# Softplus in one activation, exponentials in groups, and a new order for an attention and MLP kernel

## The chip, the cores and the metric

The kernel runs on one core of a Trainium2 chip. The metric is the device time of one execution in microseconds (us). Below, PE is TensorE, DVE VectorE, ACT ScalarE, POOL GpSimd and SP SyncE, which here only issues DMAs.

## The reference

Eight batches of eight heads: tokens `x` (512 x 64 a head) and a state (32 x 64 a head) read each other by softmax attention. The 544 rows of each batch go through a two-layer MLP whose activation is softplus.

```python
scores = scale * np.matmul(x, state.transpose(0, 1, 3, 2))       # x reads the state
a = np.exp(scores - scores.max(-1, keepdims=True)); a /= a.sum(-1, keepdims=True) + 1e-09
xread = np.matmul(a, state)
scores2 = scale * np.matmul(state, x.transpose(0, 1, 3, 2))      # the state reads x
a2 = np.exp(scores2 - scores2.max(-1, keepdims=True)); a2 /= a2.sum(-1, keepdims=True) + 1e-09
sread = np.matmul(a2, x)
rows = np.concatenate([xread, sread], axis=2)                    # -> (4608, 512)
h = rows @ w_in                                                  # 512 x 2048
g = np.maximum(h, 0.0) + np.log1p(np.exp(-np.abs(h)))            # softplus
out = g @ w_out                                                  # 2048 x 512
```

The weights come as 64-bit floats, and the kernel turns them into 32-bit ones on the chip.

## The kernel before, in words

Most products are made exact enough by splitting each fp32 operand into a high part (a cast to fp32r) and a low part (the rest) and adding three products, `PASSES` (line 27): high by high, high by low, low by high. `split` (line 86) does this: the cast on ACT or POOL, the subtraction on DVE or POOL; the table `MOVED` (line 40) says which. The early score products, the products with the weights and the transposes run in plain fp32.

The attention of the tokens is folded into the weights: V = state x w_in (per batch and head) is made first, so that GEMM 1 multiplies the transposed attention weights `aT` by V (`gemm1`, line 471: six products of 512 columns into one of two PSUM banks `h`). `softplus` (line 460) turns the tile into g: Abs, Exp and Ln on ACT, then max(h, 0) + t on DVE, and a split into `ghi` and `glo`, three buffers each. `gemm2` (line 482) adds twelve products into four banks `acc`. One tile of 128 columns of w_in is a slot; there are 16 slots a batch, and `flush` (line 545) runs a slot's GEMM 2 once three slots are pending. The state's rows of all batches go through the same MLP together near the end (`gemm1_read`, line 518), and the last batch closes the run.

`as_f32` (line 104) converts a weight piece: Prelu on ACT makes the high word (line 111), DVE shifts the low word (line 114) and joins the two (line 115). `make_v0` makes the first 512 columns of V for batches 0 to 3 from half-width pieces (lines 158 and 167), `make_vf` the others (lines 200 and 211), and `make_v` those of the later batches. `attention` is a generator of steps named by a letter and a head group 0 or 1: Q scores (line 341), A a transposition, M maximum, subtraction and exponential, N normalisation, D the transposed weights `aT`, E the exponential of the state's scores, G its transposes on PE (line 392), R the reading of x by the state (line 405), X its scaling. Batches 0 and 1 run in plain fp32 (`whole`), the others with split operands.

The order is written out by hand in strings that `run` (line 603) reads: `START` for batches 0 and 1 with all weight preparation, a `BLOCK` for each batch from 2 on, `LAST` for the last. `|` is a slot of GEMM 1, `g` a flush, `a b c` a step of attention of a batch, `v V U` steps of V, `W` a w_out piece, `i o` a load ahead, `p F` a split or a load of V. `LOADS` sets the first loads and `ATT` the order of the steps. A scheduler then places the instructions on each engine's queue; each engine works its queue in order, and all DMAs are issued from SP's queue.

Of the kernel before, what the change touches and what calls it, by code (L numbers as in the profile page):

```python
# [47 lines left out]
def attention_then_softplus_mlp(ctx: ExitStack, tc, xn, xt, zq, zp, stk, w_in, w_out, out):  # L48
# [55 lines left out]
    def as_f32(t, tag="wt"):  # L104
        if t.dtype != I64:
            return t
        v = t.bitcast(I32).rearrange("p (n t) -> p n t", t=2)
# [8 lines left out]
        return r
# [595 lines left out]
```

## Time and profile before

| | us |
|---|---|
| median of 3 runs | 708.37 (706.07 to 711.12) |
| the profiled execution | 708.3, span 706.3 |
| PE, ACT, DVE, POOL busy | 680.7, 501.3, 466.3, 172.8 |
| mean granted clock of PE | 0.995 |

The span runs from the first to the last instruction of the trace. Busy time is the union of an engine's instructions; a matmul's end is modelled. The granted clock is a share of 2.4 GHz, so 0.50 is 1.2 GHz. In an x count a plain fp32 product stands as two records.

### The profile page before, as it was taken

What the parts mean: (1) busy time and instruction counts of PE and PEld (TensorE: products, weight loads), DVE (VectorE), ACT (ScalarE), POOL (GpSimd) and SP (SyncE); (2) the same over time, 40 slices, a digit from 0 to 9 for tenths busy, and PEclk for the clock granted to TensorE, in tenths of its full rate; (3) what the DMA queues carried; (4) which work ended last, traced back from release to release, by engine and by line L of the source; (5) the groups of instructions that cost most, each with busy time, mean ns of one, the idle gap of its engine ahead of it and who ended that gap; (6) DMA issues with size and microseconds to landing.
All of it is one profiled execution on the core that took longest, in us unless ns stands there. A gap on an engine that the chain in (4) does not pass through costs nothing.

```text
span 706.3 us, 9196 instructions
## 1 busy us (share of the span) xinstructions
PE 680.7 (96%) x3012; PEld 536.0 (76%) x3012; DVE 466.3 (66%) x818; ACT 501.3 (71%) x914; POOL 172.8 (24%) x170
## 2 busy tenths in 40 slices
PE   5679999999999999999999999999999999999997
PEld 2455666888877878778777887888788888888876
DVE  4499768936798997796858754875487534544322
ACT  2588988766588778799878856875687556657452
POOL 1221102665233565201201070107010510000220
PEclk9999999999999999999999999999999999999999
DMA  8768896221335456354433311320111013412001
GB/s 267 239 246 287 265 306 199 74 61 48 96 104 164 149 162 204 105 198 153 132 92 108 103 52 38 104 75 14 47 60 59 5 58 104 143 52 60 1 0 59
DMA packets 42063, 82.91 MB, mean 117 GB/s; under 512 B 6176, under 2 KB 13088, under 8 KB 42016
## 3 DMA queue, kind: packets, MB, share of 16 engines
q1 hardware_dynamic: 42016, 82.33, 36.3%
q8 instruction: 23, 0.38, 0.2%
q14 instruction: 24, 0.20, 0.1%
HBM read 56.62 MB, written 25.69 MB: 117 GB/s over the span
## 4 chain that ended last, share of the span: by engine, by line
PE 81%; ACT 9%; DVE 7%; issue 2%; DMA 1%; POOL 0%; SPq 0%; ACTq 0%; DVEq 0%; POOLq 0%
PE acc L485 47%; PE h L478 22%; PE h L525 3%; PE aux L235 2%; PE aux L411 1%; ACT t L463 1%; ACT t L462 1%; ACT t L464 1%; ACT ghi L90 1%; PE aux L341 1%; PE aux L347 1%; DVE k L91 1%; PE aux L392 1%; DMA xT<-in_xt_dram 1%; PE aux L200 1%
## 5 line engine op out<-in xcount | busy, mean ns | idle before, releaser
L485 PE MATMUL acc<-wout,ghi 128*128 128x512 f32 x1088 | 343.1, 394 | 0.9 <-DVE StK L577 0.5
L485 PEld LDWEIGHTS acc<-wout,ghi 128*128 128x128 f32 x1088 | 203.2, 188 | 48.2 <-issue 2.4
L485 PE MATMUL acc<-wout,glo 128*128 128x512 f32 x544 | 214.1, 394 | 0.0
L478 PE MATMUL h<-aT,vhl 128*128 128x512 f32 x768 | 203.7, 402 | 4.3 <-DVE t L465 3.8
L478 PEld LDWEIGHTS h<-aT,vhl 128*128 128x128 f32 x768 | 142.2, 189 | 44.4 <-DVE t L465 9.6
L465 DVE SCALAR_TENSOR_TENSOR t<-h,t 128x512 f32<-128x512 f32 x136 | 93.1, 686 | 97.4 <-ACT t L464 97.1
L462 ACT ACTIVATE t<-h 128x512 f32<-128x512 f32 x136 | 81.4, 598 | 77.4 <-DVE glo L91 37.7
L485 PEld LDWEIGHTS acc<-wout,glo 128*128 128x128 f32 x544 | 102.1, 188 | 22.7 <-issue 0.7
L91 DVE TENSOR_TENSOR glo<-t,ghi 128x512 fp32r<-128x512 f32 x100 | 70.3, 703 | 35.4 <-ACT ghi L90 14.8
L90 ACT CAST ghi<-t 128x512 fp32r<-128x512 f32 x104 | 64.5, 620 | 36.4 <-PE acc L485 23.2
L464 ACT ACTIVATE t<-t 128x512 f32<-128x512 f32 x136 | 86.2, 634 | 2.8
L463 ACT ACTIVATE t<-t 128x512 f32<-128x512 f32 x136 | 86.3, 634 | 2.2
L91 DVE TENSOR_TENSOR vhl<-vf,vhl 128x512 fp32r<-128x512 f32 x62 | 47.1, 760 | 36.0 <-ACT vhl L90 34.0
L83 POOL TENSOR_SCALAR ghi<-t 128x512 fp32r<-128x512 f32 x32 | 21.7, 679 | 180.7 <-PE acc L485 139.8
L91 POOL TENSOR_TENSOR glo<-t,ghi 128x512 fp32r<-128x512 f32 x36 | 48.5, 1351 | 49.6 <-ACT ghi L90 43.1
L90 ACT CAST vhl<-vf 128x512 fp32r<-128x512 f32 x59 | 36.4, 616 | 18.1 <-PE h L525 11.7
L368 POOL TENSOR_TENSOR T<-T,sm 128x512 f32<-128x512 f32 x13 | 15.1, 1160 | 120.7 <-DVE sm L367 92.3
L111 ACT ACTIVATE k<-k 128x512 f32<-128x512 f32 (+1 forms) x32 | 20.2, 645 | 10.3 <-DMA k<-in_w_in_dram 7.7
L525 PEld LDWEIGHTS h<-sreadT,vhl 128*128 128x128 f32 x192 | 23.6, 191 | 2.4 <-DVE t L465 2.2
L525 PE MATMUL h<-sreadT,vhl 128*128 128x256 f32 x192 | 24.9, 286 | 0.1
L352 DVE TENSOR_TENSOR k<-aux,k 64x512 f32<-64x512 f32 x24 | 16.4, 682 | 12.5 <-ACT k L351 12.3
L115 DVE SCALAR_TENSOR_TENSOR wt<-k,wt 128x512 int32<-128x512 int32 (+1 forms) x26 | 20.2, 791 | 2.0 <-ACT k L111 1.7
(161 smaller groups left out, 697.6 us busy)
## 6 DMA issues: line engine op xcount, KB each, us to landing
vd<-ve SPq DMA_DIRECT2D x44, 256.0 KB, 3.0
xT<-in_xt_dram SPq DMA_DIRECT2D x16, 512.0 KB, 4.1
x<-in_xn_dram SPq DMA_DIRECT2D x16, 512.0 KB, 3.8
k<-in_w_out_dram SPq DMA_DIRECT2D x16, 512.0 KB, 4.8
vf<-vd SPq DMA_DIRECT2D x64, 128.0 KB, 2.6
k<-in_w_in_dram SPq DMA_DIRECT2D x12, 512.0 KB, 4.7
out_dram<-o SPq DMA_DIRECT2D x24, 256.0 KB, 2.0
wt<-wsc SPq DMA_DIRECT2D x16, 256.0 KB, 2.9
```

Of the source, the lines that this page charges most:

```text
L83: nc.gpsimd.tensor_scalar(dst, src, 1.0, 0.0, ALU.mult, ALU.add)
L90: nc.scalar.copy(hi, src)
L91: vec(*what).tensor_tensor(lo, src, f32(hi), ALU.subtract)
L111: nc.scalar.activation(h2, f32(hi), AF.Prelu, scale=2.0 ** -112, alpha=-(2.0 ** 32))
L115: nc.vector.scalar_tensor_tensor(u, h2.bitcast(I32), 3, u, ALU.logical_shift_left, ALU.bitwise_or)
L462: nc.scalar.activation(t, h, AF.Abs)
L463: nc.scalar.activation(t, t, AF.Exp, scale=-1.0)
L464: nc.scalar.activation(t, t, AF.Ln, bias=1.0)
L465: nc.vector.scalar_tensor_tensor(t, h, 0.0, t, ALU.max, ALU.add)
L478: nc.tensor.matmul(h, Vhl[b, ft // 2][:, vi, g, cs], aT[b][:, ai, g], start=(n == 0), stop=(n == 5))
L485: nc.tensor.matmul(acc[c], g[gi][:, c0:c0 + P], wout[ft][:, wi], start=(ft == first and i == 0), stop=(ft == last and i == 2))
L525: nc.tensor.matmul(h[:, 256 * i:256 * i + 256], Whl[u, i][:, wi, kt, :], sreadT[:, si, kt, :], start=(n == 0), stop=(n == 11))
```

## The change

- `softplus` is one ACT instruction with the function Softplus, reading PSUM; Abs, Exp, Ln and the DVE instruction go. Softplus is in another table set of ACT than the exponential and Prelu, so the compiler puts an `ACT_TABLE_LOAD` wherever the queue changes between them. There are 44 in the new order, against the one that line 50 places before; a late batch has six.
- In `attention` the exponential of M becomes a step of its own, `m`, and that of E a step `e`, so that the order can put a batch's four exponentials close together. `sc` and `e2` share a tag, and both groups' `a2T` lie in one buffer.
- `as_f32` keeps Prelu for pieces made before the first slot of GEMM 1, and for three that `MOVED` names. The 24 later ones take Copy (or POOL for two of them) and two DVE instructions on the 16-bit quarters of the words, into a separate buffer, before the join.
- Eight products of 128 x 128 zeros run on PE first (`WARM`); nothing reads their result. `rouse` is defined and not called.
- `LOADS`, `ATT`, `START`, the blocks, `LAST` and `MOVED` are new. 22 more casts of `ghi` and 16 more subtractions of `glo` are on POOL.

The products are the same in number and shape, the eight of zeros aside.

```diff
+WARM = 8
-LOADS = (('t', 0), ('z', 0), ('w', 0), ('w', 0), ('t', 1), ('w', 0), ('w', 0), ('w', 0), ('q', 0), ('w', 0), ('w', 0), ('q', 1), ('w', 0))
+LOADS = (('z', 0), ('t', 0), ('w', 0), ('w', 0), ('t', 1), ('w', 0), ('w', 0), ('w', 0), ('q', 0), ('w', 0), ('w', 0), ('q', 1), ('w', 0))
-START = 'aavvaaavaaavaavgavaaBoaWaboapbaaobaWvaa|ibvgVbiVoWVbVVVpbiVbbV|bbaVipWo|iVbbggVVV|VoWiiWpbgVV|VbioVb|Vgbpigo|g|Vbb|WpgbgW|oVVi|VVVVVViiVg|bVpg|pWVo|WVVVgVoVVVo|VWgVpV|WiVgo|Vgg|gpop|g|CgV|VoVgcW|ppcg|og|cW|VcVgoWVW|pVcgcpgg|ccc|cgFgccc|gcccc|pcccp|ccgc|cgc'
+START = 'vvaavaaaavvaaaaaavvaavaaaaBpbW|bbvbobVbbbbvbbWV|bbbbVVWVaVVabVaaaaaaabbbVabp|bbipogbWVgbVoVib|VpVbiW|WgbbV|VbVgiViopbgV|oibg|W|WVgVV|ogbpbi|VipVVVVg|VVWi|pVgbVg|Vg|ooVV|VVVVVVgipV|WVVWVpo|Wggo|CgoVo|cgpc|ggcpW|g|V|WgcVoVpW||WVggpcpgcgccVc||cgcc|gccccgcc|cocccpcFc|ccp|gcgcc'
...
+    if WARM:
+        idle = sb("sr", [P, P], bufs=2)
+        nc.vector.memset(idle, 0.0)
+        pb = aux()
+        for _ in range(WARM):
+            nc.tensor.matmul(pb[:, 0:P], idle, idle, start=True, stop=True)
...
-        nc.scalar.activation(h2, f32(hi), AF.Prelu, scale=2.0 ** -112, alpha=-(2.0 ** 32))
         r = sb(tag, [P, n], bufs=2 if tag == "wt" else 1)
-        u = r.bitcast(I32)
-        nc.vector.tensor_scalar(u, lo, 29, None, ALU.logical_shift_right)
-        nc.vector.scalar_tensor_tensor(u, h2.bitcast(I32), 3, u, ALU.logical_shift_left, ALU.bitwise_or)
+        if early[0] or ("pre",) + what in MOVED:
+            nc.scalar.activation(h2, f32(hi), AF.Prelu, scale=2.0 ** -112, alpha=-(2.0 ** 32))
+            u = r.bitcast(I32)
+            nc.vector.tensor_scalar(u, lo, 29, None, ALU.logical_shift_right)
+        else:
+            if ("h2",) + what in MOVED:
+                nc.gpsimd.tensor_scalar(h2, f32(hi), 2.0 ** -112, 0.0, ALU.mult, ALU.add)
+            else:
+                nc.scalar.activation(h2, f32(hi), AF.Copy, scale=2.0 ** -112)
+            u = sb("k2", [P, n], I32, bufs=K2)
+            vh = t.bitcast(U16).rearrange("p (n t) -> p n t", t=4)
+            uh = u.bitcast(U16).rearrange("p (n t) -> p n t", t=2)
+            nc.vector.tensor_scalar(uh[:, :, 0], vh[:, :, 1], 13, None, ALU.logical_shift_right)
+            nc.vector.tensor_scalar(uh[:, :, 1], vh[:, :, 3], 0x8000, None, ALU.bitwise_and)
+        nc.vector.scalar_tensor_tensor(r.bitcast(I32), h2.bitcast(I32), 3, u, ALU.logical_shift_left, ALU.bitwise_or)
...
+            elif what == "m":
+                T = v["T"]
                 nc.scalar.activation(T, T, AF.Exp, scale=SCALE)
...
+                v["nm"] = nm
+            elif what == "e":
+                nm = v["nm"]
+                e2 = v["e2"] = sb("sc", [P, S], bufs=2) if whole else v["sc"]
+                rs = v["rs"] = sb("rs", [P, 1], bufs=4)
                 nc.scalar.activation(e2, v["sc"], AF.Exp, bias=nm, scale=SCALE, accum_out=rs)
...
-        nc.scalar.activation(t, h, AF.Abs)
-        nc.scalar.activation(t, t, AF.Exp, scale=-1.0)
-        nc.scalar.activation(t, t, AF.Ln, bias=1.0)
-        nc.vector.scalar_tensor_tensor(t, h, 0.0, t, ALU.max, ALU.add)
+        nc.scalar.activation(t, h, AF.Softplus)
```

The tables move instructions on every engine. Three places in the start show it. In the rows, `h` tiles are GEMM 1 (line 478 before, 513 now), `acc` tiles with `ghi` GEMM 2 (485 and 520), `x,a2T` the reading of batch 0's state (405 before), `xT,Z` the scores of a batch (341 and 369), `ident` the transposes.

PE, from the transposes of batch 0 to the first GEMM 2, before:

```order
L392 MATMUL h_279<-ident,e_53_226 128x128 x2
L405 MATMUL acc_292<-x_204,a2T_284 128x256 x4
L392 MATMUL acc_302<-ident,e_66_266 128x128 x4
L405 MATMUL h_309<-x_206,a2T_307 128x256 x4
L341 MATMUL aux_316<-xT_257,Z_73 128x512 x2
L439 MATMUL h_344<-ident,sr_114 128x128 x4
L478 MATMUL h_357<-aT_113,vhl_297 128x512 x6
L478 MATMUL h_469<-aT_113,vhl_297 128x512 x6
L158 MATMUL acc_334<-wt_330,QZ_87 128x256
L167 MATMUL acc_338<-wt_330,wout_2_88 128x256
L485 MATMUL acc_550<-wout_68_271,ghi_369 128x512 x2
```

and now:

```order
L425 MATMUL acc_300<-ident,sc_227 128x128 x4
L425 MATMUL h_307<-ident,sc_232 128x128 x4
L513 MATMUL h_337<-aT_156,vhl_319 128x512 x3
L513 MATMUL h_408<-aT_156,vhl_319 128x512 x2
L369 MATMUL aux_324<-xT_315,Z_84 128x512 x2
L513 MATMUL h_337<-aT_156,vhl_319 128x512 x3
L513 MATMUL h_408<-aT_156,vhl_319 128x512 x3
L369 MATMUL aux_360<-xT_317,Z_84 128x512 x2
L513 MATMUL h_408<-aT_156,vhl_319 128x512
L513 MATMUL h_544<-aT_156,vhl_541 128x512 x6
L520 MATMUL acc_574<-wout_84_327,ghi_346 128x512
```

The reading of the state (`x,a2T`) is no longer there. Both score products of batch 1 and a third group of GEMM 1 (`h_544`) stand ahead of the first GEMM 2.

ACT, from the first slot's activation to the cast of its `ghi` and a little beyond (lines 462 to 464 are the old softplus, line 500 the new one, `k` a weight conversion, `sc` and `T` exponentials of batch 1), before:

```order
L462 ACTIVATE t_364<-h_357 128x512
L90 CAST sreadT<-h_344 64x2x32
L463 ACTIVATE t_364<-t_364 128x512
L464 ACTIVATE t_364<-t_364 128x512
L90 CAST sreadT<-h_344 64x2x32
L361 ACTIVATE T_375<-T_375 128x512
L111 ACTIVATE k_86_321<-k_76_290 128x512
L111 ACTIVATE k_88_328<-o_108 128x256
L90 CAST sreadT<-h_344 64x2x32
L90 CAST ghi_369<-t_364 128x512
```

and now:

```order
L500 ACT_TABLE_LOAD
L500 ACTIVATE t_344<-h_337 128x512
L413 ACT_TABLE_LOAD
L413 ACTIVATE sc_383,rs_384<-aux_324,nm_352 128x512
L129 ACTIVATE k_86_330<-k_85_328 128x512
L105 CAST ghi_346<-t_344 128x512
L391 ACTIVATE T_350<-T_350 128x512
L413 ACTIVATE sc_389,rs_390<-aux_360,nm_380 128x512
L500 ACT_TABLE_LOAD
L500 ACTIVATE t_415<-h_408 128x512
```

A load, an exponential of batch 1 and a conversion stand between the first softplus and its cast, and two more exponentials and a load before the second softplus.

DVE, around the join of the first w_out piece (`wt_331`, line 142; `k_85` is the piece as loaded, `aux_360` the second scores of batch 1), now:

```order
L131 TENSOR_SCALAR wt_331<-k_85_328 128x512
L383 STREAM_TRANSPOSE T_375<-aux_360 128x512
L406 TENSOR_REDUCE nm_380<-aux_360 128x1
L387 TENSOR_REDUCE mx_377<-T_375 128x16
L407 TENSOR_SCALAR nm_380<-nm_380 128x1
L414 TENSOR_SCALAR rs_384<-rs_384 128x1
L388 TENSOR_TENSOR T_375<-T_375,mx_377 128x512
L142 SCALAR_TENSOR_TENSOR wt_331<-k_86_330,wt_331 128x512
L106 TENSOR_TENSOR glo_347<-t_344,ghi_346 128x512
```

Before, the join of this piece (`wt_274`) stood here:

```order
L355 STREAM_TRANSPOSE T_375<-aux_316 128x512
L376 TENSOR_REDUCE nm_542<-aux_316 128x1
L114 TENSOR_SCALAR wt_274<-k_64_261 128x512
L91 TENSOR_TENSOR sreadT<-h_344,sreadT 64x2x32
L115 SCALAR_TENSOR_TENSOR wt_274<-k_69_272,wt_274 128x512
L359 TENSOR_REDUCE mx_400<-T_375 128x16
L91 TENSOR_TENSOR sreadT<-h_344,sreadT 64x2x32
```

The join stands behind four operations on the second scores of batch 1, where it had only the first scores' around it.

## Rows read from the trace of the kernel before

**Rows 1.** The page's head and first part: engine, busy us, share, instructions.

```profile
span 706.3 us, 9196 instructions
PE 680.7 (96%) x3012; PEld 536.0 (76%) x3012; DVE 466.3 (66%) x818; ACT 501.3 (71%) x914; POOL 172.8 (24%) x170
```

**Rows 2.** Busy time by stretch; columns: stretch, length, each engine's busy us, PEclk, DMA share, GB/s.

```profile
0.00:44.00 44.00, 27.49 (x81) 17.04 (x81) 23.18 (x60) 21.31 (x49) 9.21 (x14) 0.92 0.74 251
44.00:60.00 16.00, 15.05 (x52) 8.78 (x50) 13.80 (x28) 15.07 (x30) 3.50 (x4) 1.00 0.77 260
60.00:141.00 81.00, 79.69 (x313) 56.64 (x312) 67.68 (x110) 69.36 (x133) 19.41 (x17) 1.00 0.69 223
141.00:283.00 142.00, 139.81 (x628) 112.82 (x627) 112.20 (x190) 104.47 (x191) 67.63 (x64) 1.00 0.39 124
283.00:565.00 282.00, 281.33 (x1261) 226.21 (x1260) 195.33 (x353) 212.87 (x383) 58.90 (x56) 1.00 0.26 84
```

**Rows 3.** The chain of work that ended last, 141 to 160 us: start, us, what.

```profile
150.71 2.72 PE acc L485 x12
```

**Rows 4.** PE's timeline, first 60 us: start, us, what [idle before <-releaser].

```profile
4.95 3.75 PE L341 MATMUL aux<-xT,Z 128*128 128x512 f32 x4 [4.95 <-DMA Z<-in_zp_dram]
...
26.50 3.68 PE L405 MATMUL acc<-x,a2T 128*128 128x256 f32 x8 [1.60 <-ACT a2T L395]
...
33.17 1.88 PE L341 MATMUL aux<-xT,Z 128*128 128x512 f32 x4
...
35.25 1.63 PE L478 MATMUL h<-aT,vhl 128*128 128x512 f32 x6
40.11 2.84 PE L478 MATMUL h<-aT,vhl 128*128 128x512 f32 x6 [3.23 <-DVE t L465]
...
43.88 0.81 PE L485 MATMUL acc<-wout,ghi 128*128 128x512 f32 x2
```

**Rows 5.** Busy time by stretch, PE at the lower clock.

```profile
28.00:30.00 2.00, 2.00 (x6) 1.47 (x5) 0.00 (x0) 0.00 (x0) 0.00 (x0) 0.50 0.88 139
```

**Rows 6.** Instructions by line and form: line, engine, operation, names, shapes, xcount | busy, mean ns.

```profile
L465 DVE SCALAR_TENSOR_TENSOR t<-h,t 128x512 f32<-128x512 f32 x136 | 93.1, 686 | 97.4 <-ACT t L464 97.1
L463 ACT ACTIVATE t<-t 128x512 f32<-128x512 f32 x136 | 86.3, 634 | 2.2
...
L462 ACT ACTIVATE t<-h 128x512 f32<-128x512 f32 x136 | 81.4, 598 | 77.4 <-DVE glo L91 37.7 <-PE h L478 30.7 <-POOL glo L91 8.4
...
L90 ACT CAST ghi<-t 128x512 fp32r<-128x512 f32 x104 | 64.5, 620 | 36.4 <-PE acc L485 23.2 <-DVE t L465 11.6 <-PE h L478 0.9
L91 POOL TENSOR_TENSOR glo<-t,ghi 128x512 fp32r<-128x512 f32 x36 | 48.5, 1351 | 49.6 <-ACT ghi L90 43.1 <-PE aux L235 5.3
...
L83 POOL TENSOR_SCALAR ghi<-t 128x512 fp32r<-128x512 f32 x32 | 21.7, 679 | 180.7 <-PE acc L485 139.8 <-DVE t L465 21.5 <-DVE sm L365 16.8
...
L115 DVE SCALAR_TENSOR_TENSOR wt<-k,wt 128x512 int32<-128x512 int32 x24 | 19.5, 821 | 2.0 <-ACT k L111 1.7
L111 ACT ACTIVATE k<-k 128x512 f32<-128x512 f32 x28 | 18.5, 675 | 2.7 <-DMA k<-in_w_out_dram 2.4 <-DMA k<-in_w_in_dram 0.2
...
L114 DVE TENSOR_SCALAR wt<-k 128x512 int32<-128x512 int32 x24 | 11.5, 488 | 2.3 <-PE aux L211 2.2
...
L380 ACT ACTIVATE e<-k,nm 128x512 f32<-128x512 f32 x12 | 8.6, 716 | 1.6 <-DVE nm L377 1.6
...
L50 ACT ACT_TABLE_LOAD x1 | 1.3, 1283 | 0.7 <-PEq L696 0.7
```

**Rows 7.** DVE's timeline, first 46 us.

```profile
13.33 0.72 DVE L355 STREAM_TRANSPOSE T<-aux 128x512 f32<-128x512 f32 x1 [1.70 <-PE aux L341]
```

**Rows 8.** POOL's timeline, first 60 us.

```profile
25.36 1.26 POOL L91 TENSOR_TENSOR aT<-k,aT 128x512 fp32r<-128x512 f32 x1
```

**Rows 9.** The issues of SP's queue, first 60 us: start, us of issue, what.

```profile
27.90 0.43 SPq L97 DMA_DIRECT2D k<-in_w_out_dram  x1
```

**Rows 10.** The page's sixth part: what, queue, xcount, KB each, us to landing.

```profile
k<-in_w_out_dram SPq DMA_DIRECT2D x16, 512.0 KB, 4.8
```

More of the change, by code (lines that the diff above doesn't have):

```diff
@@ L13 @@
 I64 = mybir.dt.int64
+U16 = mybir.dt.uint16
 AF = mybir.ActivationFunctionType
@@ new lines @@
+START = 'vvaavaaaavvaaaaaavvaavaaaaBpbW|bbvbobVbbbbvbbWV|bbbbVVWVaVVabVaaaaaaabbbVabp|bbipogbWVgbVoVib|VpVbiW|WgbbV|VbVgiViopbgV|oibg|W|WVgVV|ogbpbi|VipVVVVg|VVWi|pVgbVg|Vg|ooVV|VVVVVVgipV|WVVWVpo|Wggo|CgoVo|cgpc|ggcpW|g|V|WgcVoVpW||WVggpcpgcgccVc||cgcc|gccccgcc|cocccpcFc|ccp|gcgcc'
+BLOCK = 'BggUbbUb|pU|UUUUbU|UbUbbgb|Fp|gbbFpUbggg|UbbpUFFbbUUUbb|gg||pbgbbUbbUpbbUggUbgU|bU||b|U|bgUpgpUUUbUgU|UUU|'
+BLOCK2 = 'BUU|g|bpg|UUbbbUUbbFbbUUppUbgbUb|gbgb|FFg||bUbbUbpggUUbb|bFbb|UggbpUUbb|gUpbgUggUUU|pUbU|U|UUgbUg|UUbU|pU|'
@@ L77, in attention_then_softplus_mlp, with rouse @@
     make_identity(nc, ident)
+    if WARM:
[4 more added lines that the diff above has]
+            nc.tensor.matmul(pb[:, 0:P], idle, idle, start=True, stop=True)
+    def rouse():
+        pb = aux()
+        for c in range(4):
+            nc.tensor.transpose(pb[:, P * c:P * c + P], ident, ident)
     def vec(*what):
@@ L98, in load_w, with as_f32 @@
         return t
-    def as_f32(t, tag="wt"):
+    def as_f32(t, *what, tag="wt"):
         if t.dtype != I64:
@@ L154, in make_v0 @@
                 k = 4 * half + q
-                wt = as_f32(first.pop(0), tag=f"wout{4 + k}" if k < 6 else "wt")
+                wt = as_f32(first.pop(0), 0, half, q, tag=f"wout{4 + k}" if k < 6 else "wt")
                 nc.sync.dma_start(wsc[0][P * q:P * q + P, cs], wt)
@@ L195, in make_vf @@
             for q in range(4):
-                wf = as_f32(ahead("in"), tag="wout12" if (4 * c + q) % 3 == 2 else "wt")
+                wf = as_f32(ahead("in"), c, q, tag="wout12" if (4 * c + q) % 3 == 2 else "wt")
                 nc.sync.dma_start(wsc[c][P * q:P * q + P, :], wf)
@@ L310, in load_z @@
         nc.sync.dma_start(t, zp[b])
-        z = sb("zhl", [P, 4, 2, 64], F32R, bufs=2)
+        z = sb("zhl", [P, 4, 2, 64], F32R, bufs=1)
         split(z[:, :, 0], z[:, :, 1], t)
@@ L342, in attention @@
             elif what == "Q":
-                sc = v["sc"] = sb("k2", [P, S], bufs=K2)
+                sc = v["sc"] = sb("sc", [P, S], bufs=2)
                 for j in range(2):
@@ L363, in attention @@
                 T = v["T"]
-                sm = sb("sm", [P, 16], bufs=1)
+                sm = sb("mx", [P, 16], bufs=1)
                 nc.vector.tensor_reduce(sm, T, AX.X, ALU.add)
@@ L393, in attention @@
                 if whole:
-                    v["a2T"] = sb("a2T", [P, S], bufs=1)
-                    nc.scalar.copy(v["a2T"], pb)
+                    both = t[1 - g].get("both") or sb("a2T", [P, 2, S], bufs=1)
+                    v["both"] = both
+                    v["a2T"] = both[:, g]
+                    if ("a2T", b, g) in MOVED:
+                        nc.vector.tensor_copy(v["a2T"], pb)
+                    else:
+                        nc.scalar.copy(v["a2T"], pb)
                 else:
@@ L456, in split_wout @@
         wout[ft] = sb(f"wout{ft}", [P, 2, DM], F32R)
-        w = as_f32(ahead("out"))
+        w = as_f32(ahead("out"), ft)
         split(wout[ft][:, 0], wout[ft][:, 1], w, "wout", ft)
@@ L624, in run @@
                 load_ahead({"i": "in", "o": "out"}[what])
+            elif what == "d":
+                rouse()
             elif what == "g":
```

12 lines of the change are left out of this document (4 added, 8 removed).

## The prediction

> **What bounds the kernel now.** Read the page's first part first: PE is busy 680.7 of 706.3 us, ACT 501.3 and DVE 466.3 [rows 1]. The change takes work from ACT and DVE, so it can pay only where PE waits for them. The windows by stage come next [rows 2], because a share of the whole hides where that is. From 283 to 565 us PE is busy 281.33 of 282, and there is nothing to remove. From 141 to 283 it is idle 2.2 us, from 60 to 141 it is idle 1.3, from 44 to 60 it is idle 0.95. In the first 44 us it is busy 27.49 and idle 16.5, at a granted clock of 0.92. Where PE is dense, twelve products take 2.72 us, 227 ns each [rows 3], and nothing in the change makes these fewer or shorter. The start is nearly all there is to win.
>
> PE's timeline of the start shows how the time goes there [rows 4]. The first score product takes 3.75 us and the same shape 1.88 at 33.17, so it ran at half speed. From 26.50 PE reads batch 0's state, eight records in 3.68 us, with the granted clock at 0.50, which is 1.2 GHz, after a stretch in which it had mostly stood [rows 5]. The first group of GEMM 1 starts only at 35.25, the second waits 3.23 us for the DVE end of the first softplus, and GEMM 2 starts at 43.88.
>
> **The change part by part.** *Softplus.* Three ACT instructions of 598, 634 and 634 ns (the third has the second's row again) and one of DVE of 686 become one on ACT [rows 6], 136 times. No row shows the new function. It is worth at least the 598 ns of the first, which reads the same tile, and at most the 1.87 us of all three. I take 0.6, since it is one pass with one input and one output of the same shape. ACT loses 272 x 634 ns = 172 us, DVE 136 x 686 ns = 93 us. The Trainium skill ("ScalarE: Activation LUTs", Step-by-step: what each stage is for) says that an activation's rate is one element per cycle whatever the function; by it the estimate is about 0.6 as well, and no run here shows it yet.
>
> *Table loads.* The order has 44 where one stood. One is 1283 ns [rows 6], so 43 more are 55 us on ACT. Together with 22 casts of 620 ns that go to POOL, ACT comes to about 370 us. In a late batch (212.87 us in 282 [rows 2], so 54 in 72) it loses 2 x 16 x 634 ns = 20 us and gets six loads, 7.7 us, and stays far from PE's 72. There the loads are free while PE has products queued, which is the third rival.
>
> *Halves.* 24 late weight pieces are converted by two DVE instructions and a join in place of one and a join. The one takes 488 ns now [rows 6]. Each half has as many elements, but narrower ones, so an added instruction costs between nothing (in the shadow of another) and the join's 821 ns. I take 0.49, or 12 us on DVE over some 100 us. The 93 that leave hide it: for each slot of GEMM 1 DVE has 0.69 back. Without that cover 0.5 us would lie on each piece. POOL gets 22 casts of 679 ns and 16 subtractions of 1351, 37 us on an engine that is busy 172.8 of 706.3.
>
> *Unread products.* Eight small ones run from the first us, while PE waits 4.95 us for the first load [rows 4]; there they cost nothing. If they leave the clock high, a score product shrinks by 1.9 us. DVE waited 1.70 us for the second one's result at 13.33 [rows 7], so at most 1.7 can reach the chain. DVE also has weight pieces to convert there, so I take 1.0, with 0 and 1.7 as ends.
>
> *New order, the main term.* GEMM 1 of batch 0 now stands directly behind the transposes, and the reading of batch 0's state goes behind part of GEMM 2's third slot. By the first product of GEMM 2 the new order has passed on PE one more weight piece (0.9), the second score product of batch 1 (1.88) and a third group of GEMM 1 (1.36): 4.1 us. It has left out 16 records of reading (3.7 at full clock, half of 2 x 3.68) and four transposes (0.4): 4.1 us. The work is equal, so the difference in GEMM 2's start is the lead:
>
> (a) The second half of batch 0's attention weights is ready at 25.36 + 1.26 = 26.6 now [rows 8]. The new order puts two more half-width weight pieces ahead of it on DVE, each half of 488 + 821 ns, so 1.3 together; less the 1.0 from above that is 27 (25 to 28.5).
> (b) PE then has five products of GEMM 1 and batch 1's first score product behind it. Six more products (1.4) and the second score product (1.88) end at 30.3. A spell at half clock, as at 26.50 now, adds up to 2; I take 1: 31.3.
> (c) ACT: the first softplus ends at 29.0. The order then sets a load (1.28), an exponential of batch 1 (0.72), a weight conversion (0.68) and the cast (0.62) ahead of GEMM 2: 32.3.
> (d) GEMM 2 also needs the first w_out piece. Its load is issued at 27.90 now; the new order has it ahead of all loads of x, at 26 to 27, and 4.8 us later it has landed [rows 9, 10]. On DVE four operations of batch 1's second scores (some 0.65 each) stand ahead of its join, and they wait for (b): 31.3 + 2.6 + 0.82, then POOL's cast of 0.68: 35.4.
>
> The last, (d), sets it: 35.4, with ends at 31 and 41. The lead is 43.9 - 35.4 = 8.5 us.
>
> Is it kept? Up to the third softplus ACT has five table loads (6.4 us), four exponentials, four conversions and some seven casts or copies, 16 us from about 28.5 on, so the third tile is cast at about 45.5. PE's own work up to there is two slots of GEMM 2, a group of GEMM 1, two pieces of the next columns and half a group: 2 x 2.72 + 1.36 + 2 x 1.72 + 0.9 = 11.1, which ends at 46.5. The cover is 1 us, so the term lies close to its edge. On SP the loads of batch 0's x go behind further weight loads; the reading that waits for them has gone behind too, so I cost that at nothing, and without that cover PE would stand for about one landing. The DMA share of 0.74 and 0.77 up to 60 us [rows 2] leaves room to fetch the same weights 9 us earlier. Of the 3.5 us that PE is idle between 60 and 283 I take 1.0 back, since ACT and DVE have more slack there; the ends are 0 and 3.5.
>
> **Sum.** The profiled execution took 708.3 us, 2.0 more than its span, and the median of the three runs is 708.37, the same. 708.3 - 8.5 - 1.0 = 698.8, or 699. About 1%, 7.1 us, is what a measurement of this kernel can tell from no change; the forecast is just beyond it.
>
> **The rivals.** *A switch costs more than its load* (0.19). ACT may have to run empty before a load, and the one load in the trace stands behind no work. If a switch costs two loads, the five in the start add 6.4 us ahead of the third tile; 1 us is covered, and the lead shrinks to 3.1. The late batches still hold, at 54 - 20 + 15 = 49 of 72. That gives 704. The Trainium skill ("ScalarE: Activation LUTs", What ACT_TABLE_LOAD costs) states 1283 ns, as the row has it, and about 1380 ns of draining besides for every switch to another set; by that the estimate is 705. For this rival speaks that the new order switches right where the cover is 1 us. Against it, ACT's instructions there wait for each other anyway.
>
> *Softplus is as long as the three* (0.08), so that the change doesn't do what its name says. Then 1.27 us lie on each of the first three slots, 3.8 less the 1 of cover, and nothing is won later: 703. Against it speaks that the ACT rows of this shape lie between 598 and 716 ns [rows 6], whatever the function.
>
> *The switches stop PE in the late batches* (0.12), the case on the other side. The order there is load, exponential, load, softplus. The exponential waits for DVE's maximum, and the softplus stands behind it in the queue while its tile holds one of GEMM 1's two banks. A pair takes 1.28 + 0.72 + 1.28 + 0.6 = 3.9 us, and PE has two slots of GEMM 2 and a group of GEMM 1 queued, 6.8 us. It decides from an exponential that waits over 2.9 us on. If each of the 21 pairs then costs 1 us, 21 are lost: 720. At 0.45 us a pair the gain is gone. Against it: ACT and DVE are lighter there, and GEMM 1's bank is now free after one ACT instruction, not after three and one of DVE.
>
> *The lead is larger* (0.05): GEMM 2 at 31 and all of the later 3.5 us: 692, and with half of the 44 to 60 idle time and a shorter reading, down to 688.
>
> **How the numbers follow.** The forecast has 0.56, and its bounds that matter are 692 to 701. Faster by over 1% (below 701.3): 0.56 + 0.05 = 0.61. Within 1%: the first two rivals, 0.27. Slower (above 715.5): 0.12. The range runs from the larger lead past the first two rivals to the unchanged 708: 688 to 708, with the 0.12 outside.
>
> **What would show it.** GEMM 2's first product near 35 and not 43.9; PE idle some 8 us in the first 36; table loads of 1.28 us with little idle time around them; six of them in a late batch with PE still busy over 99%. If GEMM 2 starts at 35 and the third tile's cast is well behind 47, it is the switches. Gaps of PE in the late batches that end on a softplus would show the third rival. If GEMM 2 starts after 41, step (a) or (d) is wrong.

## The result, and the profile after

The changed kernel takes 698.94 us (median of 4 executions, 698.25 to 700.30) beside 707.38 for the kernel before (4, 706.07 to 711.12): a ratio of 0.9875 [0.9832, 0.9918]. Two later comparisons gave 700.13 beside 709.12, 0.9871 [0.9848, 0.9895], and 700.83 beside 708.11, 0.9901 [0.9883, 0.9918]. I had forecast 699.0. The profiled execution took 700.3 us, and its span is 698.5.

The page's head and first part, for [rows 1]:

```profile
span 698.5 us, 8899 instructions
...
PE 677.0 (97%) x3028; PEld 536.8 (77%) x3028; DVE 396.4 (57%) x692; ACT 386.3 (55%) x653; POOL 219.4 (31%) x217
```

ACT lost 115 us and DVE 70, and the kernel is 8 us shorter. Busy time by stretch, with the columns of [rows 2]:

```profile
0.00:44.00 44.00, 32.27 (x113) 20.33 (x114) 32.06 (x79) 28.48 (x57) 6.36 (x13) 1.00 0.75 252
44.00:60.00 16.00, 14.21 (x62) 10.04 (x61) 15.92 (x35) 14.10 (x27) 3.44 (x4) 1.00 0.89 293
60.00:141.00 81.00, 79.91 (x314) 57.53 (x313) 54.68 (x88) 53.69 (x96) 29.25 (x26) 1.00 0.63 215
141.00:283.00 142.00, 139.59 (x624) 111.71 (x623) 103.73 (x174) 85.01 (x142) 70.89 (x67) 1.00 0.40 130
283.00:565.00 282.00, 281.91 (x1273) 229.03 (x1273) 159.44 (x278) 162.59 (x264) 89.61 (x90) 1.00 0.25 83
```

In the first 44 us PE is idle 11.7 us, where it was idle 16.5. From 44 to 60 DVE is now busy for 15.92 of 16 us: the work of the start has moved forward, and DVE is full there. Equal times are not equal work, though, so a second measure is needed: at what time does the n-th product of GEMM 2 start? Both kernels issue the same 1632. These starts are read from PE's timelines (n counted from 0; a late batch is 192 products):

| kernel (profiled execution) | n=0 | 132 | 192 | 768 | 960 | 1152 | 1344 | 1630 |
|---|---|---|---|---|---|---|---|---|
| before | 43.88 | 127.06 | 146.38 | 384.04 | 455.98 | 527.89 | 608.19 | 701.86 |
| after | 38.01 | 120.46 | 141.45 | 376.75 | 448.01 | 519.36 | 600.65 | 694.05 |
| e1, one unread product | 38.14 | 122.04 | 143.03 | 377.53 | 448.78 | 520.13 | 601.37 | 694.78 |
| e2, old softplus in the new order | 36.18 | 124.05 | 146.35 | 394.47 | 470.74 | 546.47 | 626.54 | 724.04 |
| e3, new softplus in the old order | 44.40 | 135.98 | 155.30 | 392.24 | 463.99 | 535.79 | 616.85 | 711.94 |
| e4, Prelu for all pieces | 38.86 | 123.67 | 145.53 | 381.61 | 452.89 | 524.29 | 605.56 | 698.95 |
| e5, after again | 39.72 | 122.54 | 143.53 | 378.58 | 449.85 | 521.23 | 602.49 | 695.89 |
| e6, w_out piece first | 35.72 | 123.33 | 144.31 | 379.02 | 450.22 | 521.55 | 602.84 | 696.24 |
| e7, earlier still | 35.71 | 122.87 | 143.86 | 378.95 | 450.21 | 521.55 | 602.79 | 696.20 |
| e8, bank and t wait for DVE | 36.93 | 124.00 | 144.99 | 381.57 | 453.47 | 525.15 | 606.54 | 699.79 |
| e9, bank alone | 37.74 | 122.13 | 143.08 | 379.75 | 451.64 | 523.37 | 605.02 | 698.32 |
| e10, t alone | 38.34 | 124.73 | 145.72 | 381.01 | 452.39 | 523.75 | 604.80 | 698.18 |
| e11, unread in the wait | 37.42 | 119.31 | 140.30 | 379.12 | 450.38 | 521.72 | 602.98 | 696.38 |
| e12, after once more | 37.19 | 121.42 | 142.41 | 376.74 | 448.00 | 519.35 | 600.63 | 694.04 |

Equal n is not yet equal work, because other products stand between those of GEMM 2. At product 192 the lead reads 4.93, but the changed kernel has by then passed 126 products of GEMM 1 and the kernel before 120, and six of these are 1.36 us where PE is dense [rows 3]. At products 132 and 1344 both have passed the same products of every kind, the zeros aside, so the 7.81 us between the first two lines at the end are divided there. At 132 the lead is 6.60. From there to 1344 the kernel before takes 481.13 us and the changed one 480.19, so 0.94 are won, and 0.27 behind it. The two late batches from 768 to 1152, which hold the same products in both, take 143.85 and 142.61: they win 1.24, and the rest of that stretch loses 0.3. The three profiled executions of the changed kernel spread over 2.1 us at product 132 (leads of 6.60, 4.52 in e5 and 5.64 in e12), and one of them stays 1.84 behind to the end.

Instructions by line and form, for [rows 6]: line, engine, operation, names, shapes, count | busy us, mean ns | idle time before and what ended it.

```profile
L500 ACT ACTIVATE t<-h 128x512 f32<-128x512 f32 x136 | 81.2, 599 | 133.8 <-POOL glo L106 51.9 <-PE h L513 50.1 <-DVE glo L106 28.2
...
L500 ACT ACT_TABLE_LOAD x22 | 28.2, 1283 | 1.5 <-PE h L513 1.1
...
L140 DVE TENSOR_SCALAR k<-k 128x512 uint16<-128x512 uint16 x24 | 14.6, 610 | 0.7 <-DMA k<-in_w_out_dram 0.6
...
L141 DVE TENSOR_SCALAR k<-k 128x512 uint16<-128x512 uint16 x24 | 13.9, 579 | 0.0
```

Softplus takes 599 ns, the same as Abs on the same tile. The two halves take 610 and 579 ns in the mean where the one shift took 488 [rows 6]. Their medians are 452 and 453 ns, and 422 for the shift: a few of over a microsecond, up to 1.57, raise the means.

### The profile page after: what moved, and what is told of

Read it like the earlier page. It is cut to its first block, busy times and chain, and to the rows that moved or that the text cites. A ratio compares the mean times of both kernels' runs of the same rounds, so it can differ in the third digit from the quotient of the medians.

```text
span 698.5 us, 8899 instructions
## 1 busy us (share of the span) xinstructions
PE 677.0 (97%) x3028; PEld 536.8 (77%) x3028; DVE 396.4 (57%) x692; ACT 386.3 (55%) x653; POOL 219.4 (31%) x217
## 3 DMA queue, kind: packets, MB, share of 16 engines
q1 hardware_dynamic: 42016, 82.33, 35.7%
## 4 chain that ended last, share of the span: by engine, by line
PE 79%; DVE 9%; DMA 4%; ACT 4%; issue 2%; POOL 2%; SPq 0%; ACTq 0%; DVEq 0%; POOLq 0%
PE acc L520 46%; PE h L513 22%; PE h L560 4%; PE aux L262 1%; PE aux L375 1%; PE aux L449 1%; PE aux L227 1%; PE aux L238 1%; DVE glo L106 1%; DMA xT<-in_xt_dram 1%; DMA k<-in_w_out_dram 1%; DMA k<-in_w_in_dram 1%; DMA wt<-wsc 1%; DVE wt L142 1%; PE aux L425 1%
## 5 line engine op out<-in xcount | busy, mean ns | idle before, releaser
L106 DVE TENSOR_TENSOR glo<-t,ghi 128x512 fp32r<-128x512 f32 x84 | 63.0, 750 | 110.4 <-ACT ghi L105 59.4
L106 POOL TENSOR_TENSOR glo<-t,ghi 128x512 fp32r<-128x512 f32 x52 | 69.5, 1337 | 128.0 <-ACT ghi L105 100.6
L98 POOL TENSOR_SCALAR ghi<-t 128x512 fp32r<-128x512 f32 x54 | 37.1, 688 | 144.3 <-PE acc L520 48.1
L105 ACT CAST ghi<-t 128x512 fp32r<-128x512 f32 x82 | 50.8, 620 | 55.6 <-PE acc L520 54.5
L98 POOL TENSOR_SCALAR vhl<-vf 128x512 fp32r<-128x512 f32 x15 | 10.1, 674 | 70.5 <-PE h L513 66.6
L500 ACT ACT_TABLE_LOAD x22 | 28.2, 1283 | 1.5 <-PE h L513 1.1
L106 DVE TENSOR_TENSOR k<-xT,k 128x512 fp32r<-128x512 f32 x22 | 20.8, 944 | 6.1 <-ACT k L105 5.7
L277 DVE TENSOR_TENSOR R<-wt,R 64x512 fp32r<-64x512 f32 x24 | 22.2, 925 | 3.5 <-ACT R L276 2.9
L276 ACT CAST R<-wt 64x512 fp32r<-64x512 f32 x24 | 14.9, 619 | 15.8 <-PE aux L262 7.2
L106 DVE TENSOR_TENSOR k<-x,k 128x512 fp32r<-128x512 f32 x19 | 16.9, 889 | 8.8 <-ACT k L105 4.4
L262 PE MATMUL aux<-R,StK 128*128 128x512 f32 x64 | 19.9, 403 | 2.0 <-DVE ve L265 1.3
```

What stands on the lines that cost most here:

```text
L106: vec(*what).tensor_tensor(lo, src, f32(hi), ALU.subtract)
L262: nc.tensor.matmul(pb, StK[i][:, h, :], r, start=(i == 0), stop=(i == 1))
L276: nc.scalar.copy(r[a], wf[a])
L277: vec("R", *what, o).tensor_tensor(r[z], wf[a], f32(r[a]), ALU.subtract)
L500: nc.scalar.activation(t, h, AF.Softplus)
```

## The experiments

Each edit is against the changed kernel unless it says otherwise. e1 to e4 ran beside the kernel before at 708.62 us, e5 to e8 at 709.12, e9 to e12 at 708.11. An edit also lets the scheduler place other instructions anew: up to product 192, e1 and the unedited e5 and e12 have the changed kernel's order on every engine, and e2, e4 and e6 to e11 do not.

**e1: one unread product in place of eight.**

```diff
-WARM = 8
+WARM = 1
```

> The changed kernel with one unread product at the start in place of eight. Theory A (the products keep the clock high and that reaches the path): the first two score products go back from 2.42 and 1.98 us to about 3.7 and 3.5, spells at 1.2 GHz come back around 25 to 40 us, GEMM 2 starts 1 to 3 us after 38.0, and the whole is 1 to 3 us longer (700 to 702 us). Rival B (DVE, ACT and the loads cover it): the score products are slower, GEMM 2 starts within 0.5 us of 38.0, and the whole is the same within 0.7 us.

Measured: 700.58 us, 0.9886 [0.9859, 0.9913]. GEMM 2 starts at 38.14. The first two score products take 3.75 and 3.58 us, against 2.42 and 1.98 behind eight unread ones. The granted clock reads 1.00 there in both runs, so only the durations speak for a low clock. They make the first product of GEMM 1 0.8 us later (26.19 against 25.37). Batch 1's second scores, which wait for xT in both, start at 31.78 and 31.65, and so take it back. From 36 to 44 us the granted clock is 0.58; it is down there in e5 (0.78) and e12 (0.79) too, with eight unread products. At product 192 the run lies within the spread of the unedited kernel. The unread products are worth nothing that shows.

**e2: the old softplus in the new order.**

```diff
-        nc.scalar.activation(t, h, AF.Softplus)
+        nc.scalar.activation(t, h, AF.Abs)
+        nc.scalar.activation(t, t, AF.Exp, scale=-1.0)
+        nc.scalar.activation(t, t, AF.Ln, bias=1.0)
+        nc.vector.scalar_tensor_tensor(t, h, 0.0, t, ALU.max, ALU.add)
```

> The changed kernel in its new order, with the old softplus (three ACT instructions and one of DVE), so that one table load is left. Theory A (the new order makes the lead, the single activation makes the late batches shorter): GEMM 2 still starts at 36 to 39 us, a late batch goes from 71.3 back to 71.9 us, four of them 2.4 us in all, the whole is 701 to 704 us. Rival B (the single activation makes the lead, because ACT and DVE are what fills the start): GEMM 2 starts after 41 us, and the whole is 706 us or more. Rival C (the table loads eat what the activation saves): the whole is 699 us or less.

Measured: 731.72 us, 1.0330 [1.0299, 1.0361], with one table load in all. None of my reasons gave that. GEMM 2 starts at 36.18, a lead of 7.70; at product 132 3.01 of it are left, and each late batch then takes 76 us. The weight loads of GEMM 1 from 385 to 520 us show the place:

```profile
L516 PEld LDWEIGHTS h<-aT,vhl 128*128 128x128 f32 x173 | 31.1, 188 | 16.6 <-DVE t L503 9.5 <-issue 1.1
```

and ACT's first step of the softplus in the same stretch shows what else is held:

```profile
L500 ACT ACTIVATE t<-h 128x512 f32<-128x512 f32 x29 | 17.4, 599 | 28.3 <-POOL glo L106 15.6 <-DVE glo L106 12.6
```

PE waits 9.5 us for DVE to have read `h`, since GEMM 1 has two banks. ACT waits for `glo`, since `t` has two buffers and the subtraction that makes `glo` reads the last of it. By these rows the new order leaves so little time between a tile and its use that three steps on ACT and one on DVE no longer fit.

**e3: the new softplus in the old order** (against the kernel before).

```diff
-        nc.scalar.activation(t, h, AF.Abs)
-        nc.scalar.activation(t, t, AF.Exp, scale=-1.0)
-        nc.scalar.activation(t, t, AF.Ln, bias=1.0)
-        nc.vector.scalar_tensor_tensor(t, h, 0.0, t, ALU.max, ALU.add)
+        nc.scalar.activation(t, h, AF.Softplus)
```

> The kernel before with one edit: the single softplus activation, in the old order, which the table sets cut into 60 loads. Theory A (order makes the lead): GEMM 2 starts between 42 and 46 us, the late batches stay at 71.9 us or get shorter by up to 0.6, and the whole is 704 to 712 us. Rival B (the single activation is the gain, wherever it stands): 702 us or less. Rival C (switches stop PE when exponentials are not grouped): 715 us or more, with PE gaps in the late batches that end on a softplus.

Measured: 716.37 us, 1.0110 [1.0083, 1.0137], with 60 table loads. The loss is in the start, as busy time by stretch shows:

```profile
44.00:60.00 16.00, 15.69 (x54) 10.55 (x53) 12.70 (x25) 15.63 (x27) 4.22 (x4) 0.89 0.77 227
60.00:141.00 81.00, 75.42 (x274) 50.76 (x273) 51.25 (x89) 75.34 (x118) 13.18 (x12) 0.96 0.63 220
```

ACT is busy 15.63 of 16 us and then 75.34 of 81, and PE, which was busy 79.69 of these 81, falls to 75.42. One such moment on ACT's timeline:

```profile
77.93 1.28 ACT L462 ACT_TABLE_LOAD   x1
79.23 0.60 ACT L462 ACTIVATE t<-h 128x512 f32<-128x512 f32 x1
```

and on PE's:

```profile
79.88 1.65 PE L475 MATMUL h<-aT,vhl 128*128 128x512 f32 x3 [1.77 <-ACT t L462]
```

GEMM 1 waits 1.77 us for a bank, of which the load is 1.28. The late batches take 71.75 and 71.80 us, not the 71.3 of the changed kernel. So the activation alone loses 8 us, the rest of the change without it 23, and together they win 7 to 9. Neither has a gain of its own.

**e4: Prelu for all weight pieces**, so no halves.

```diff
-        if early[0] or ("pre",) + what in MOVED:
+        if True:
```

> The changed kernel with all weight pieces converted by Prelu as before (no 16-bit halves), which brings 28 more table loads (72), all before 200 us, 36 us more on ACT, and takes 24 DVE instructions of 0.6 us away. Theory A (ACT's queue is on PE's path in the start): PE gets gaps between 40 and 140 us, and the whole is 3 to 12 us longer, 702 to 711 us. Rival B (ACT's slack of 27 in 81 us between 60 and 141 us takes the loads in): the same within 1 us, 698 to 700 us.

Measured: 704.29 us, 0.9942 [0.9923, 0.9962], where the changed kernel has 0.9871 to 0.9901: 3 to 5 us more. Prelu needs another table set than Softplus, so its line alone has 17 loads where the changed kernel has 2, and 72 stand in all. ACT's busy time from 60 to 141 us, for the row of the changed kernel above:

```profile
60.00:141.00 81.00, 78.22 (x303) 54.60 (x302) 44.36 (x71) 78.71 (x119) 18.39 (x17) 1.00 0.61 204
```

ACT is busy 78.71 us in place of 53.69. What the halves buy is not time of their own but the loads that they save at the place where ACT is fullest.

**e5: the changed kernel again**, as a yardstick for e6 to e8.

> The changed kernel itself, unedited, as the yardstick for the three kernels run beside it on this chip: 698.3 to 700.6 us by its earlier runs, GEMM 2's first product at 37.9 to 38.2 us.

Measured: 700.13 us, 0.9871 [0.9848, 0.9895]. Its profiled execution is 1.8 us longer than the first one, and PE's busy time is 680.8 us, not 677.0. Busy time by stretch shows three us of it:

```profile
33.00:36.00 3.00, 3.00 (x6) 1.35 (x5) 1.05 (x2) 1.72 (x3) 0.00 (x0) 0.50 1.01 398
```

The granted clock is 0.50, or 1.2 GHz, behind a wait of 1.98 us for xT; in the first execution that wait was 1.45 and the clock stayed at 1.00.

**e6: the first w_out piece ahead of batch 1's loads.**

```diff
-START = 'vvaavaaaavvaaaaaavvaavaaaaBpbW|...
+START = 'vvaavaaaavvaaaaaavvaavaaaaoBpbW|bbvbobV...
...
```

(only the `o` is new; the rest of the string is unchanged)

> The changed kernel with one letter of START moved: the first piece of w_out is loaded, and so joined on DVE, before batch 1's x and xT. Theory A (GEMM 2 began at 38.0 us and not at my 35.4 because its first w_out tile was joined behind batch 1's second scores, whose xT landed late, and the time won there stays to the end): GEMM 2's first product at 35 to 37 us, total 696.5 to 698 us, 1 to 2.8 us less than the changed kernel beside it. Theory B (the same, but a later wait takes it back, since batch 1's attention now comes later by as much): GEMM 2 at 35 to 37 us, total within 1 us of the changed kernel. Theory C (the queue only swaps one late transfer for another): GEMM 2 at 38 us or later, total 0 to 3 us more.

Measured: 702.48 us, 0.9900 [0.9876, 0.9924], 2.35 us more than e5. GEMM 2 does start early, and loses it again at once. PE's timeline:

```profile
35.72 1.53 PE L520 MATMUL acc<-wout,ghi 128*128 128x512 f32 x6
...
49.18 1.33 PE L227 MATMUL aux<-wout,QZ 128*128 128x512 f32 x2 [2.53 <-DVE wout L142]
...
71.15 1.12 PE L238 MATMUL aux<-wt,wout 128*128 128x512 f32 x2 [2.07 <-ACT sr L457]
```

The same two waits are 1.45 and 0.61 us in the changed kernel. The second goes back to a transfer: on ACT's timeline the scaling `sr`, for which PE waits, stands behind the conversion of a later w_out piece that has not landed.

```profile
69.50 1.24 ACT L136 ACTIVATE k<-k 128x512 f32<-128x512 f32 x2 [2.21 <-DMA k<-in_w_out_dram]
70.63 0.47 ACT L457 ACTIVATE sr<-aux,rs 128x256 f32<-128x256 f32 x1
```

In the changed kernel the same conversion waits 0.93 us. GEMM 2 began 4 us before that of e5, and at product 192 it is 0.8 behind. The queue swapped one late transfer for at least one other, as theory C had it, though the start itself moved, as A and B had it.

**e7: the same load further up.** The `o` stands among the steps of the first pieces (`...vaaaaaavovaav...`).

> The same load moved further up, among the halves of w_in. Theory A: GEMM 2 no earlier than in the run before it, since the second pair of g tiles, not w_out, would then be what it waits for; total within 0.7 us of that run. Theory B: total within 1 us of the changed kernel. Theory C: the w_in pieces behind it land 1 to 1.5 us later, the attention's start and GEMM 2 with them; total 1 to 3 us above the changed kernel.

Measured: 702.69 us, 0.9902 [0.9881, 0.9923], with GEMM 2 at 35.71: the same as e6, as theory A had it.

**e8: bank and t wait for DVE.**

```diff
         nc.scalar.activation(t, h, AF.Softplus)
+        nc.vector.tensor_tensor(t[:, 0:1], t[:, 0:1], h[:, 0:1], ALU.max)
```

> The changed kernel with one DVE operation of one column behind each softplus (t's first column is taken as the larger of t and h, which leaves it as it is), so that the bank of h stays occupied until DVE has read it, as it did before; ACT keeps its free time. It adds 136 x about 0.1 us = 14 us to DVE, which is busy 396 of 698 us. Theory A (the 0.6 us that each late batch gains comes from h's bank being free as soon as ACT has read it): late batches (GEMM 2 products #768 to #960 to #1152) at 71.7 to 72.0 us apart in place of 71.3, the total 3 to 6 us more. Theory B (the gain comes from ACT's and DVE's free time, whoever holds the bank): batches at 71.2 to 71.45 us, total 0 to 2 us more, from the start alone. Theory C (DVE's queue makes the bank late for good, the first reason of the old softplus's loss in the new order): batches at 73 us or more, total 10 us or more above.

Measured: 707.95 us, 0.9982 [0.9964, 1.0001], 7.8 us more than e5: nearly the whole gain of the change is gone. The late batches take 71.90 and 71.68 us, as before the change. The number is between theories A and C, the batches are A's. But the edit does three things at once, so the next two part them.

**e9: the bank alone.**

```diff
+        nc.vector.tensor_scalar(h[:, 0:1], h[:, 0:1], 1.0, None, ALU.mult)
```

> The changed kernel with one DVE operation of one column behind each softplus that rewrites h's first column in place (times 1): the bank of h stays occupied until DVE has been there, t is not touched, so the conversion of t does not wait for DVE. It parts what the run with t = max(t, h) did at once (+7.8 us). Theory A (the bank): 705 to 709 us, late batches 71.6 to 72.0 us apart. Theory B (t comes later to ghi): within 1.5 us of the changed kernel (699 to 702), batches 71.2 to 71.45. Theory C (DVE's queue stands still at its head until each softplus is done, and everything else behind it): 704 to 708 us here and in the next run alike.

Measured: 705.30 us, 0.9964 [0.9950, 0.9977], 4.5 more than e12.

**e10: t alone.**

```diff
+        nc.vector.tensor_scalar(t[:, 0:1], t[:, 0:1], 1.0, None, ALU.mult)
```

> The same with the DVE operation on t's first column alone (times 1): t is late, h's bank is free as soon as ACT has read it. Theory A (the bank): within 1.5 us of the changed kernel, batches 71.2 to 71.45. Theory B (late t): 705 to 709 us, batches 71.6 to 72.0. Theory C (DVE's queue): 704 to 708 us here and in the run on the bank alike.

Measured: 704.09 us, 0.9942 [0.9925, 0.9958], 3.3 more than e12. The two numbers are alike, as theory C had it, and the places are not. e10's late batches are those of the changed kernel (71.38 and 71.36 us; PE is busy 281.91 of the 282 us from 283 to 565); of its 4.1 us at the end 3.3 are there by product 192 (145.72 against 142.41 in e12). e9 is only 0.7 behind e12 at product 192, 3.0 at 768, 4.0 at 1152: it loses in every batch (71.89 and 71.73; PE busy 280.19). Both put the same wait at the head of DVE's queue, 115.4 us in all in e10 and 114.0 in e9, as the row of e9's new operation shows:

```profile
L501 DVE TENSOR_SCALAR h<-h 128x1 f32<-128x1 f32 x136 | 22.2, 163 | 114.9 <-ACT t L500 114.0
```

Where PE loses shows better in its weight loads, since a product's end is modelled. Here are those of GEMM 1 in the two late batches (products 768 to 1152): count, busy us, mean ns, and idle us before them with what ended it. In e9, 379.75 to 523.37 us:

```profile
L514 PEld LDWEIGHTS h<-aT,vhl 128*128 128x128 f32 x192 | 35.3, 188 | 9.9 <-DVE h L501 2.4 <-DVE rs L415 0.4
```

and in e10, 381.01 to 523.75 us:

```profile
L514 PEld LDWEIGHTS h<-aT,vhl 128*128 128x128 f32 x192 | 35.2, 188 | 9.2 <-ACT t L500 2.0
```

The changed kernel has 8.9 us there (the row stands further down). So in the new order a bank that DVE must free as well costs about 0.5 us a late batch, and a late t costs nothing there. What the scheduler placed anew between these products (22 of PE's 644 in e9, 10 in e10) has not been parted from it. In e10's start it can't be the bank. That this loss is DVE standing still where it was full (15.92 of 16 us) fits the rows; a lower clock up to 36 us in that execution (0.91) and the new places of instructions have a part in it, and I have not parted them.

**e11: unread transposes in the wait before GEMM 2.**

```diff
     def rouse():
-        pb = aux()
+        pb = bank("acc", 4)
...
-...bbbVabp|bbipogbWVg...
+...bbbVabp|bbipoddddgbWVg...
```

> The changed kernel with 4 times 4 unread transposes of the identity issued around GEMM 2's start; three groups of them (about 1.9 us) stand in the wait of 2.76 us that ends at 38.0 us. Theory A (that wait is what drops the granted clock in some executions: 0.78 over 36 to 44 us in one of them, with 3.8 us more of PE busy time): clock 1.0 over 36 to 44 us, total 0.5 to 1.5 us less than the changed kernel beside it. Theory B (the clock falls at waits before it, or the wait is the same later on): total within 0.5 us. Theory C (the transposes stand in the way of GEMM 1 or GEMM 2): 0.5 to 2 us more.

Measured: 701.55 us, 0.9908 [0.9888, 0.9927], beside e12's 0.9901: no difference that can be told. PE's timeline has the transposes in the wait, which is now 1.22 us and not 2.76:

```profile
34.72 1.47 PE L92 MATMUL acc<-ident 128*128 128x128 f32 x12
37.42 1.42 PE L520 MATMUL acc<-wout,ghi 128*128 128x512 f32 x5 [1.22 <-POOL wout L98]
```

From 36 to 44 us the clock is 1.00 (0.79 in e12), and up to product 192 this execution leads e12 by 2.1. At product 768 it is 2.4 behind. Most of that is one place on PE's timeline:

```profile
255.41 0.73 PE L262 MATMUL aux<-R,StK 128*128 128x512 f32 x2 [2.70 <-DVE ve L265]
```

and DVE's timeline names what DVE waited for:

```profile
254.66 0.69 DVE L265 COPY ve<-aux 128x512 f32<-128x512 f32 x1 [1.73 <-DMA vd<-ve]
```

The copy of a V tile waits for the store of an earlier one out of the same buffer. In e12 the wait at that place is 0.90. Behind it the granted clock falls to 0.61 from 258 to 261 us.

A gain of the start met a transfer that it had not set. This is one execution; whether the wait is there in most is open.

**e12: the changed kernel once more.**

> The changed kernel, unedited, beside the three others: 699 to 701 us.

Measured: 700.83 us, 0.9901 [0.9883, 0.9918].

## Why the prediction came out right, and where its steps did not

The number held: the sum was 698.8 for a profiled execution that took 700.3. That the median of 698.94 lies on the forecast of 699.0 is luck: the later comparisons gave 700.13 and 700.83, and the main term was too large while one that I had put at nothing was not.

**Softplus.** 0.6 us was right, and 599 ns the measure. By the rule of the Trainium skill that I weighed there ("ScalarE: Activation LUTs", Step-by-step: what each stage is for) it would have been the same; the trace agrees. ACT at 386 us is near my 370.

**Table loads.** 44 loads of 1283 ns, with 1.5 us of idle time before the 22 of softplus and 0.2 before each of the groups of the exponentials. ACT's timeline shows two switches in a row:

```profile
28.29 1.28 ACT L500 ACT_TABLE_LOAD   x1
29.58 0.60 ACT L500 ACTIVATE t<-h 128x512 f32<-128x512 f32 x1
30.20 1.28 ACT L413 ACT_TABLE_LOAD   x1
31.49 0.69 ACT L413 ACTIVATE sc<-aux,nm 128x512 f32<-128x512 f32 x1
...
33.45 0.61 ACT L105 CAST ghi<-t 128x512 fp32r<-128x512 f32 x1
33.96 0.64 ACT L391 ACTIVATE T<-T 128x512 f32<-128x512 f32 x1
```

A load starts 0.02 us after the activation ahead of it ends, and the next activation 0.01 after the load. The cast and the exponential behind it, with no load between, overlap by 0.1 us (33.45 + 0.61 against 33.96), so a switch costs the load and that overlap. My first rival, a switch at two loads, falls. So does, for this kernel, what the Trainium skill ("ScalarE: Activation LUTs", What ACT_TABLE_LOAD costs) states on draining, about 1380 ns beside each load: no row has it. What a load does cost the kernel differs: its full length at the place shown in e3, 3 to 5 us for 28 of them in e4, and nothing that shows in the changed kernel's late batches.

**The main term, 8.5 us.** GEMM 2 starts at 38.01, not at 35.4. PE's timeline:

```profile
25.37 1.44 PE L513 MATMUL h<-aT,vhl 128*128 128x512 f32 x5
26.65 1.88 PE L369 MATMUL aux<-xT,Z 128*128 128x512 f32 x4
28.05 2.15 PE L513 MATMUL h<-aT,vhl 128*128 128x512 f32 x6
31.65 1.98 PE L369 MATMUL aux<-xT,Z 128*128 128x512 f32 x4 [1.45 <-DMA xT<-in_xt_dram]
33.07 2.19 PE L513 MATMUL h<-aT,vhl 128*128 128x512 f32 x7
38.01 1.43 PE L520 MATMUL acc<-wout,ghi 128*128 128x512 f32 x5 [2.76 <-POOL wout L98]
```

DVE's timeline, the join of the w_out piece:

```profile
36.19 0.68 DVE L142 SCALAR_TENSOR_TENSOR wt<-k,wt 128x512 int32<-128x512 int32 x1
```

Step (d) had the chain right: scores, four operations, join, cast on POOL. The step that failed is (b), by 2.3 us: the second scores end at 33.6 and not at 31.3. PE stood 1.45 us for their xT, and I had put no DMA into that step. The cast took 0.99 us, not 0.68. So the lead at GEMM 2's first product is 5.87.

"Is it kept?" came out right in the main: at equal work the lead is 6.60 at product 132, and in the two other profiled executions 4.16 became 4.52 (e5) and 6.69 became 5.64 (e12). The cover of the third tile held. Its softplus ends at 47.0 us, POOL has cast it at 48.2, and PE takes it up at 51.58 without a wait for it. (My own terms give 28.5 + 16 = 44.5 for that cast, not 45.5.) But an early start by itself is not a lead. e6 has the 35.7 that I had forecast, and of its 8.16 us 3.73 are left at product 132; e2 has 3.01 left of 7.70. What counts is the lead at equal work behind the stretch in which pieces, V and tiles all arrive. The term is 6.6, not 8.5.

**Unread products, 1.0.** 0.8 at the first product of GEMM 1 and nothing that shows at GEMM 2's (38.14 in e1 against 37.19 to 39.72 with eight), the lower end that I had kept. I had not looked for a transfer behind the chain that takes it back.

**Later idle time, 1.0.** From 60 to 283 us PE is idle 3.5 us as before (1.09 and 2.41), so its idle time did not fall where I had looked. 0.94 is won between products 132 and 1344, and the two late batches alone make 1.24.

**"Nothing to remove" in the late batches.** Wrong by 0.6 us a batch. PE's busy share of 99.8% does not show it, because the waits are short and a product's end is modelled. The count of records in the same 282 us does: 1261 before [rows 2], 1273 after. The idle time before the weight loads shows where. In the two late batches before, 384.04 to 527.89 us:

```profile
L485 PEld LDWEIGHTS acc<-wout,ghi 128*128 128x128 f32 x257 | 47.8, 188 | 11.0 <-ACT o L135 1.0
L478 PEld LDWEIGHTS h<-aT,vhl 128*128 128x128 f32 x192 | 35.3, 188 | 9.2 <-DVE t L465 1.8
...
L392 PEld LDWEIGHTS aux<-ident,e 128*128 128x128 f32 x16 | 1.7, 141 | 1.0 <-ACT e L380 1.0
```

and now, 376.75 to 519.36 us:

```profile
L520 PEld LDWEIGHTS acc<-wout,ghi 128*128 128x128 f32 x256 | 47.5, 188 | 10.2 <-DVE o L160 0.2 <-ACT o L162 0.2
L513 PEld LDWEIGHTS h<-aT,vhl 128*128 128x128 f32 x192 | 35.2, 188 | 8.9 <-ACT t L500 1.7
...
L425 PEld LDWEIGHTS aux<-ident,sc 128*128 128x128 f32 x16 | 2.0, 140 | 0.6
```

Of the 1.5 us that are gone, 0.8 stood ahead of GEMM 2, 0.4 ahead of the transposes and only 0.3 ahead of GEMM 1. So the bank of `h`, which e9 shows must not be held longer, is the smaller part of the gain. The waits that went ended on ACT's copies of the accumulators (`o`) and its exponential (`e`), and ACT is busy 162.59 of the 282 us where it was busy 212.87. I had counted ACT's slack for 60 to 283 us alone. That the slack by itself does it is not shown: e3 has ACT at 178.19 in the old order, and its batches take 71.75 and 71.80.

**Halves.** 0.6 us each in the mean and 0.45 in the median, for my 0.49, hidden as I said. Their worth, 3 to 5 us (e4), lies in the 28 loads that don't stand there; I had costed the halves and not their absence.

**The case on the other side**, switches that stop PE in the late batches, did not come: PE is busy 281.91 of 282 us there, with six loads a batch. In the old order (e3) the switches do stop PE, in the start.

In sum: 8.5 became 6.6, and "1.0 later, 0 in the batches" became 1.2 (0.94 + 0.27), of which the two late batches of the table make 1.24 by themselves. 708.3 - 6.6 - 1.2 = 700.5, and the profiled execution took 700.3.

## What to carry to other kernels

The first consumer's start is not a lead: measure it where both kernels have done the same work of every kind, behind the last stretch in which inputs still arrive, and ask of each transfer that you move forward which one it pushes back. Busy shares near 100% hide short waits; the idle time before the weight loads names them. An experiment that takes a gain back has not yet shown where the gain came from: holding a bank costs as much a batch as the change won, and most of that was won elsewhere. An activation from another table set paid here when the order grouped its neighbours by set; try the operation and the order together, since each alone can lose.
